# First matmuls of seven products over pairs of token groups, 512 columns each

## The chip, the core and the metric

The program runs on one core of a Trainium2 chip. A core has a matrix engine (TensorE, PE in the profile), a vector engine (VectorE, DVE), an activation engine (ScalarE, ACT), a general engine (GpSimd, POOL) and a queue engine that here only issues transfers (SyncE, SP). PE multiplies a stationary 128x128 tile, which a separate weight load (PEld) puts into the array, by a moving tile, and writes to PSUM, eight banks of 512 fp32 columns by 128 partitions. The other engines read PSUM and work on SBUF. The metric is the device time of one execution in microseconds (us), as the median of several runs.

## The reference

Batch 8, 8 heads, 576 positions, head size 64; then 4608 tokens of width 512 and 8 experts of hidden size 1024. Every expert is applied to every token; the routing only gives weights.

```python
def phi(x):
    proj = einsum('bhsd,df->bhsf', x, w_phi)
    proj = proj - max(abs(proj), axis=-1)
    return concatenate([exp(proj), exp(-proj)], -1)
q_p, k_p = phi(q), phi(k)
num = einsum('bhsf,bhfd->bhsd', q_p, einsum('bhsf,bhsd->bhfd', k_p, v))
x = (num / den).transpose(0, 2, 1, 3).reshape(4608, 512)

P = exp(x @ w_gate - max)
for _ in range(8):
    P /= P.sum(1); P /= P.sum(0); P *= N / E
for e in range(8):
    h = maximum(x @ w1[e], 0)          # the first matmul of an expert
    out += P[:, e:e+1] * (h @ w2[e])   # the second matmul
```

## The kernel before

**Stages.** The attention part ends at about 206 us and leaves x transposed in `xT` (four 128-row blocks of the width by 4608 tokens, bf16). Tokens are worked in nine groups `g` of 512. Expert 0 runs in the plain way (`up0`, `down0`), until 254 us, while DVE and PE find the routing weights `P`. Then experts 1 to 7 follow with a scheme of seven products.

**Seven products.** A product of two matrices, each cut in 2x2 blocks, is made from seven block products instead of eight; for that, sums of blocks of both factors are needed, and sums of the products. In the first matmul (`up7`) the two block columns of x are the two halves of a group, 256 tokens each. The seven products are called x1, y1, x2, w1, x3, x4, w2, each for two parts `fp` of the hidden size (x10 is x1 of part 0). `product` (L1075 to L1087) issues one of them as two blocks `i` of 128 hidden rows by two steps `k`: four matmuls of 256 columns. ACT copies a partial result from PSUM to a tile `U` (`keep`, L1112) or applies the relu (L1121); DVE adds PSUM and `U` and clips at zero (`add`, L1116, called CUSTOM_DVE_ANT_0 in the profile and ISA in the program's order). The result goes to tiles `hT`, two of 4 KB a partition for each group.

The second matmul (`down7`) has the products X1, Y1, Z1, X2, X3, Z2, X4, each of eight matmuls of 256 columns. DVE makes four sums `S` of blocks of `hT` first (`sub`, L992, four instructions of 1024 elements). Results are scaled by `P` and added to the fp32 accumulator `acc` of the group: X2, Z2 and X4 by two DVE instructions each (L1231), X1, Y1, Z1 and X3 by two ACT instructions into a tile `V` (L1243) and one POOL addition (L1246).

**Sums of x.** Four sums per group are made once, at expert 1 (`sums_x`), by DVE in instructions of 512 elements, stored to DRAM (`Xd`) and loaded again for each expert, two transfers of 256 KB a group (`load_x`, L1074), into three tiles `X`. SP issues them.

**Order.** Nothing runs in the order in which it is written. Each call of `pe`, `act`, `dve`, `pool` or `dma` records an operation with an assumed duration and its dependences; `Plan.schedule` then takes, again and again, the operation that can start first by those durations (ties by the order of writing), and fixes with it the sequence of each engine. Tiles and banks are handed out in the same pass. Each engine works through its sequence strictly, so an instruction that waits holds up all behind it on that engine. The list `ORDER` says how the second matmul of a group is written between the products of the first matmul of the next.

**The end.** For expert 7 the groups come as 8, 0, ..., 7. The last, group 7, takes its second matmul in the plain way (`down8`): 24 matmuls of 512 columns and 16 of 256, and five DVE instructions that scale and add (L1179), each followed by a store.

Of the kernel before, what the change touches and what calls it, by code (L numbers as in the profile page):

```python
# [228 lines left out]
def kernel(  # L229
# [37 lines left out]
    colw = const.tile([128, 128], FP32, name="colw")  # L267
    xT = const.tile([128, NP, N], BF16, name="xT")
    L = const.tile([128, NT, E], FP32, name="L")
# [47 lines left out]
    ring(hp, [128, 4, 512], BF16, "hT", 4)  # L317
# [22 lines left out]
    ring("s_p", [128, 1024], BF16, "T", 9)  # L340
# [3 lines left out]
    ring("s_p", [128, 2, 2, 256], BF16, "X", 3)  # L344
# [6 lines left out]
    def new(tag):  # L351
        return banks.new(int(tag[1])) if tag in ("P1", "P2") else R[tag].new()

# [395 lines left out]
    def up(w1, g, hT, fcs, n, r=(), w=()):  # L749

        for f0 in fcs[::n]:
            ph = new(f"P{n}")
            ht = hT[f0 // 4]
            for i in range(n):
                for dc in range(NP):
                    pe(512, lambda f=f0 + i, i=i, dc=dc, ph=ph: mm(
                        ph()[:, 512 * i:512 * i + 512], w1()[:, dc, f * 128:(f + 1) * 128],
                        xT[:, dc, g * 512:(g + 1) * 512], dc == 0, dc == NP - 1),
                        xkeys(g, dc) + [(w1, (f0 + i) // 2), *r], [ph, *w], [ht])
            act(512 * n, lambda f0=f0, ph=ph, ht=ht: nc.scalar.activation(  # L760
                out=ht()[:, f0 % 4:f0 % 4 + n, :].rearrange("p a b -> p (a b)"),
                in_=ph()[:, 0:512 * n], func=ACT.Relu, bias=0.0, scale=1.0),
                [ph], [(ht, f0 + i) for i in range(n)])

    def down(w2, hT, tss, r=()):
        py = new(f"P{len(tss)}")
        for i, ts in enumerate(tss):
            for fc in range(8):
                pe(512, lambda i=i, ts=ts, fc=fc: mm(
                    py()[:, 512 * i:512 * i + 512],  # L770
                    hT[fc // 4]()[:, fc % 4, ts * 128:(ts + 1) * 128],
                    w2()[:, fc, :], fc == 0, fc == 7),
                    [(hT[f // 4], f) for f in (range(8) if fc == 0 else (fc,))]
# [8 lines left out]
    def up0(g, part):  # L782
        if part == 0:
            hts[g] = [new("hT") for _ in range(2)]
# [123 lines left out]
    for d in plan.ops[:-1]:  # L908
        if any(b.ring in attn_rings for b in d.bufs):
            d.users.append(o)  # L910
            o.deps.append(d)
            o.left += 1

# [40 lines left out]
    routing()  # L954
    for i in fill:
# [3 lines left out]
    def store(g, ts, js=()):  # L959
        if len(js):  # L960
            cols = slice(256 * js[0], 256 * js[-1] + 256)
            dma("SP", len(js) << 17, 320, lambda: nc.sync.dma_start(
                out=out[g * S:g * S + SM].rearrange("(p j) d -> p j d", j=NJ)[:, ts:ts + 1, cols],
                in_=acc[g][:, ts:ts + 1, cols]),
                [("acc", g, ts, j) for j in js], [("out", g, ts, j) for j in js])
# [28 lines left out]
    def sums_w(e, w1, w2):  # L994
# [17 lines left out]
        def t(n):  # L1012
# [12 lines left out]
            k(w1, *a12) + [S[1]] + late, [S[3]])  # L1025
# [20 lines left out]
    def xq(g, i, j):  # L1046
# [3 lines left out]
    Xd = [[dram.tile([128, 4, 256], BF16, name=f"xd{g}{i}") for i in range(2)]  # L1050
          for g in range(NG)]

    def sums_x(g):
# [7 lines left out]
        for n, y, z, r in ((0, b12, b11, []), (1, b22, x(0), [0]), (2, b22, b12, []),  # L1061
                           (3, b21, x(1), [1])):
            sub(dve, 512, x(n), y, z, ALU.subtract,
                xkeys(g) + ["late"] + [(X[i // 2], i % 2) for i in r]
                + ([(X[1], "slot")] if n == 2 else []),
                [(X[n // 2], n % 2)] + ([(X[1], "slot")] if n == 0 else []))
        for i in range(2):
            dma("SP", 1 << 18, 250, lambda i=i: nc.sync.dma_start(out=Xd[g][i], in_=X[i]()),
                [(X[i], n) for n in range(2)], [("Xd", g, i)])

    def load_x(g):
        X = [new("X") for _ in range(2)]
        for i in range(2):
            dma("SP", 1 << 18, 250, lambda i=i: nc.sync.dma_start(out=X[i]().rearrange("p a b c -> p (a b) c"), in_=Xd[g][i]),  # L1074
                [("Xd", g, i)], [X[i], "order of X"])  # L1075
# [13 lines left out]
    def up7(A, g, X, hT, r0):  # L1089

        def b(n):
            f, r = {"11": (xq(g, 0, 1), []), "21": (xq(g, 1, 1), []), "22": (xq(g, 1, 0), []),
                    "t1": (lambda: X[0]()[:, 0], [X[0]]), "t2": (lambda: X[0]()[:, 1], [X[0]]),
                    "t3": (lambda: X[1]()[:, 0], [X[1]]),
                    "t4": (lambda: X[1]()[:, 1], [X[1]])}[n]
            return f, r

        x, y, w = ([new("P1") for _ in range(2)] for _ in range(3))
        u = [[new("U") for _ in range(2)] for _ in range(2)]

        def prod(bank, fp, x, y, first, more=(), takes=(), wk=()):
            f, r = A[x]
            rhs, r2 = b(y)
            product(bank[fp], lambda k, i: f()[:, k, 128 * (2 * fp + i):][:, 0:128],
                    lambda k: rhs()[:, k, :], 2, xkeys(g) + r + r2 + list(more), first, takes, wk)

        def out_(fp, i, j):

            return hT[i]()[:, 2 * fp:2 * fp + 2, 256 * j:256 * j + 256]
# [5 lines left out]
        def add(bank, fp, n, i, j):  # L1115
            dve(500, lambda: nc.vector._custom_dve(  # L1116
                ADD_SAT, out=out_(fp, i, j), in0=bank[fp]().rearrange("p (a b) -> p a b", a=2),
                in1=u[fp][n](), s0=3.0e38, s1=0.0), [bank[fp], u[fp][n]], [(hT[i], fp, j)])

        def relu(fp, i, j):  # L1120
            act(512, lambda: nc.scalar.activation(  # L1121
                out=out_(fp, i, j), in_=x[fp]().rearrange("p (a b) -> p a b", a=2),
                func=ACT.Relu, bias=0.0, scale=1.0), [x[fp]], [(hT[i], fp, j)])
# [4 lines left out]
        def x1(fp):  # L1128
            prod(x, fp, "11", "11", True, more, u[fp] + hT)
            keep(fp, 0)  # L1130

        def y1(fp):
            prod(y, fp, "12", "21", True, r0, hT)
# [6 lines left out]
        def w1(fp):  # L1140
            prod(w, fp, "s1", "t1", True, A["s4"][1] + r0, hT, [("banks", fp)])
# [10 lines left out]
        def w2(fp):  # L1152
# [5 lines left out]
            for fp in range(2)}  # L1158
# [4 lines left out]
    def down8(e, g, hT, w2):  # L1163

        for ts in (2, 3, 0, 1):
            halves_ = 2 if ts == 1 else 1
            n = DD // halves_
            for c in range(halves_):
                py, cols = new("P1"), slice(n * c, n * c + n)
                for fc in range(8):  # L1170
                    i, j = fc // 4, ts // 2
                    pe(n, lambda py=py, ts=ts, fc=fc, cols=cols, n=n: mm(
                        py()[:, 0:n], hT[fc // 4]()[:, fc % 4, ts * 128:ts * 128 + 128],
                        w2()[:, fc, cols], fc == 0, fc == 7),
                        [(hT[i], fp, j) for i in range(2) for fp in range(2)]
                        + [(w2, i, j) for i in range(2) for j in range(2)] + ["P"], [py])
                js = range(2) if n == DD else (c,)
                dve(580 * n // 512, lambda py=py, ts=ts, cols=cols, n=n:
                    nc.vector.scalar_tensor_tensor(  # L1179
                        out=acc[g][:, ts, cols], in0=py()[:, 0:n],  # L1180
                        scalar=P[:, 4 * g + ts, e:e + 1], in1=acc[g][:, ts, cols],
                        op0=ALU.mult, op1=ALU.add),
                    [py, "P"], [("acc", g, ts, j) for j in js])
                store(g, ts, js)

    def down7(e, g, hT, B7):


        def a(i, j):
            return lambda: hT[j]()[:, :, 256 * i:256 * i + 256]  # L1190

        def hk(i, j):
            return [(hT[j], fp, i) for fp in range(2)]

        late, seen = akey(g), set()
        S = [new("S") for _ in range(4)]
        S01 = dve
        sub(dve, 1024, lambda: S[2](), a(0, 0), a(1, 0), ALU.subtract, hk(0, 0) + hk(1, 0),
            [S[2]])
        sub(S01, 1024, lambda: S[0](), a(1, 0), a(1, 1), ALU.add, hk(1, 0) + hk(1, 1), [S[0]])  # L1200
        sub(S01, 1024, lambda: S[1](), lambda: S[0](), a(0, 0), ALU.subtract,
            [S[0]] + hk(0, 0), [S[1]])
        sub(dve, 1024, lambda: S[3](), a(0, 1), lambda: S[1](), ALU.subtract,
            [S[1]] + hk(0, 1), [S[3]])

        def prod(bank, lhs, y, r, first, more=()):
            f, r2 = B7[y]
            product(bank, lambda k, i: lhs()[:, k, 128 * i:128 * i + 128],
                    lambda k: f()[:, k, :], 4, r + r2 + (["P"] if e else late) + list(more), first)

        def start(bank, i, j):

            out_ = acc_part(g, i, j)
            w = [("acc", g, 2 * i + n, j) for n in range(2)]
            if (i, j) in seen:
                dve(500, lambda: nc.vector.tensor_tensor(
                    out=out_(), in0=bank().rearrange("p (a b) -> p a b", a=2), in1=out_(),
                    op=ALU.add), [bank] + late, w)
            else:
                act(512, lambda: nc.scalar.copy(  # L1220
                    out=out_(), in_=bank().rearrange("p (a b) -> p a b", a=2)),
                    [bank] + late, w)
            seen.add((i, j))

        def read(bank, i, j):

            if e == 0:
                return start(bank, i, j)
# [8 lines left out]
        def read2(bank, i, j):  # L1237

            if e == 0:
                return start(bank, i, j)  # L1240
            u = new("V")
            for n in range(2):
                act(390, lambda n=n: nc.scalar.activation(  # L1243
                    out=u()[:, n, :], in_=bank()[:, 256 * n:256 * n + 256], func=ACT.Copy,
                    bias=0.0, scale=P[:, 4 * g + 2 * i + n, e:e + 1]), [bank, "P"], [(u, n)])
# [14 lines left out]
        def X1():  # L1260
            prod(x, a(0, 0), "11", hk(0, 0), True, S[1:3])
            read2(x, 0, 0)

        def Y1():
            prod(y, a(0, 1), "21", hk(0, 1), True)
            read2(y, 0, 0)

        def Z1():
            prod(z, lambda: S[0](), "t1", [S[0]], True, S[3:4])
            read2(z, 1, 1)  # L1270

        def X2():
            prod(x, lambda: S[1](), "t2", [S[1]], False)
            read(x, 0, 1)

        def X3():
            prod(x, lambda: S[2](), "t3", [S[2]], False)
            read2(x, 1, 1)
# [71 lines left out]
```

## Time and profile before

| | |
|---|---|
| runs | median 1033.93 us (1033.42 to 1034.48, three runs) |
| the profiled execution | 1034.06 us, span of its instructions 1032.3 us |
| granted PE clock | 0.999 |
| PE busy | 1015.8 us, 98% |
| DVE busy | 822.8 us, 80% |
| ACT busy | 710.0 us, 69% |
| POOL busy | 464.8 us, 45% |

A busy time counts an instruction from its start to its end, and instructions of one engine overlap at their edges: a matmul of 256 columns lasts 273 ns in the profile, and the next one starts about 109 ns after it. Rates are therefore read from the distance of starts. The chain is what the profile finds by going back from the last instruction to whatever released each step.

### The profile page before, as it was taken

How to read it: one execution, taken by the hardware profiler on the slowest of the kernel's cores; microseconds unless marked ns; L12 is line 12 of the kernel's file. 1: busy time of each engine (PE TensorE's matmuls, PEld its weight loads, DVE VectorE, ACT ScalarE, POOL GpSimd, SP SyncE). 2: the span in 40 equal slices, each digit the busy share in tenths (PEclk: the TensorE clock that was granted, in tenths of full speed). 3: DMA queues.
4: the chain of work that ended last, by engine and by line, in shares of the span. 5: the costliest groups of instructions: out<-in, count | busy, mean ns of one | idle time of the engine just before them, and what ended most of it. 6: DMA issues, size and time to landing. Idle time of an engine off the chain costs nothing.

```text
span 1032.3 us, 24552 instructions
## 1 busy us (share of the span) xinstructions
PE 1015.8 (98%) x9526; PEld 843.5 (82%) x9526; DVE 822.8 (80%) x1628; ACT 710.0 (69%) x1569; POOL 464.8 (45%) x534
## 2 busy tenths in 40 slices
PE   7899999999999999999999999999999999999998
PEld 5666666645888888888888888888888888888886
DVE  7999998987777887778776877788777877787775
ACT  7999999835777756666666566666666656666663
POOL 5877765400244443334444443344444444434442
PEclk9999999999999999999999999999999999999999
DMA  9998995085411251115211441134111611114333
GB/s 247 182 173 145 180 165 95 11 204 135 93 49 42 50 115 41 42 49 99 70 42 43 91 83 42 42 83 93 41 45 50 123 43 42 42 46 129 113 134 123
DMA packets 105381, 93.93 MB, mean 91 GB/s; under 512 B 45408, under 2 KB 80544, under 8 KB 105264
## 3 DMA queue, kind: packets, MB, share of 16 engines
q1 hardware_dynamic: 71504, 68.44, 23.9%
q0 software_dynamic: 33680, 23.90, 16.4%
q8 instruction: 74, 1.21, 0.5%
q14 instruction: 43, 0.35, 0.1%
q10 hardware_dynamic: 80, 0.03, 0.0%
HBM read 94.98 MB, written 14.16 MB: 106 GB/s over the span
## 4 chain that ended last, share of the span: by engine, by line
PE 94%; DVE 3%; DMA 1%; ACT 1%; SPq 1%; issue 1%; POOL 0%; DVEq 0%
PE P L1084 73%; PE P L468 18%; PE P L667 1%; DMA acc<-in_q_dram 1%; DVE m L460 1%; PE P L706 1%; DMA v_r<-in_v_dram 1%; SPq L390 0%; PE P L672 0%; DVE S L992 0%; DVE hT L1116 0%; DVE acc L1231 0%; ACT k L464 0%; ACT q L464 0%; DVE xb L687 0%
## 5 line engine op out<-in xcount | busy, mean ns | idle before, releaser
L1246 POOL TENSOR_TENSOR acc<-acc,V 128x512 f32<-128x512 f32 x248 | 318.4, 1292 | 437.6 <-ACT V L1243 434.3
L1116 DVE CUSTOM_DVE_ANT_0 hT<-P,U 128x512 bf16<-128x512 f32 x378 | 255.3, 688 | 121.5 <-ACT U L1112 68.6
L1112 ACT COPY U<-P 128x512 f32<-128x512 f32 x378 | 216.4, 587 | 126.8 <-PE P L1084 121.7
L1243 ACT ACTIVATE V<-P 128x256 f32<-128x256 f32 x496 | 205.0, 473 | 131.1 <-PE P L1084 119.6
L1084 PEld LDWEIGHTS <-w 128*128 128x128 bf16 x2016 | 197.3, 98 | 23.1
L1084 PEld LDWEIGHTS <-S 128*128 128x128 bf16 x1984 | 194.1, 98 | 22.7 <-issue 0.3
L1231 DVE SCALAR_TENSOR_TENSOR acc<-P,acc 128x256 f32<-128x256 f32 x372 | 158.9, 478 | 58.2 <-PE P L1084 56.1
L1084 PEld LDWEIGHTS <-T 128*128 128x128 bf16 x1512 | 147.9, 98 | 18.0 <-issue 0.9
L1084 PEld LDWEIGHTS <-hT 128*128 128x128 bf16 x1488 | 145.5, 98 | 18.4 <-DVE hT L1116 1.0
L1084 PE MATMUL P<-X,w 128*128 128x256 bf16 x1008 | 154.3, 273 | 0.0
L1084 PE MATMUL P<-xT,w 128*128 128x256 bf16 x1008 | 151.1, 273 | 0.0
L1084 PE MATMUL P<-X,T 128*128 128x256 bf16 x1008 | 148.7, 273 | 0.0
L1084 PE MATMUL P<-w,hT 128*128 128x256 bf16 x992 | 142.2, 273 | 0.9 <-ACT V L1243 0.5
L1084 PE MATMUL P<-T,S 128*128 128x256 bf16 x1056 | 136.3, 273 | 0.1
L1084 PE MATMUL P<-w,S 128*128 128x256 bf16 x928 | 126.3, 273 | 0.0
L593 POOL TENSOR_TENSOR v<-v_m,em 128x512 bf16<-128x512 f32 x64 | 66.9, 1045 | 44.2 <-ACT em L464 40.0
L460 DVE TENSOR_REDUCE m<-P 128x4 f32<-128x512 f32 x128 | 83.8, 680 | 3.6 <-PE P L468 2.5
L992 DVE TENSOR_TENSOR S<-hT 128x1024 bf16<-128x1024 bf16 x124 | 84.2, 711 | 0.0
L1121 ACT ACTIVATE hT<-P 128x512 bf16<-128x512 f32 x126 | 72.9, 600 | 13.1 <-PE P L1084 12.3
L468 PE MATMUL P<-w,hT 128*128 128x512 bf16 (+1 forms) x328 | 79.5, 374 | 0.2 <-DVE m L460 0.2
L1084 PE MATMUL P<-xT,T 128*128 128x256 bf16 x504 | 75.5, 273 | 0.8 <-DVE hT L1116 0.8
L468 PE MATMUL P<-xT,w 128*128 128x512 bf16 x288 | 74.8, 379 | 0.3 <-ACT q L464 0.3
(97 smaller groups left out, 1097.8 us busy)
## 6 DMA issues: line engine op xcount, KB each, us to landing
X<-xd SPq DMA_DIRECT2D x126, 256.0 KB, 2.6
w<-in_moe_w_dram POOLq DMA_DIRECT2D x14, 1024.0 KB, 10.0
v_m<-in_v_dram SPq DMA_DIRECT2D x14, 512.0 KB, 4.4
out_dram<-acc SPq DMA_DIRECT2D x14, 512.0 KB, 3.1
xd<-S SPq DMA_DIRECT2D x18, 256.0 KB, 2.4
qk<-in_k_dram POOLq DMA_DIRECT2D x12, 256.0 KB, 5.6
qk<-in_q_dram POOLq DMA_DIRECT2D x12, 256.0 KB, 6.7
w<-in_moe_w_dram POOLq DMA_DIRECT2D x8, 256.0 KB, 7.7
```

Of the source, the lines that this page charges most:

```text
L460: dve(el, lambda: nc.vector.tensor_reduce(out=dst(), in_=src(), axis=AX.X, op=ALU.max, apply_absolute_value=True), r, w)
L468: nc.tensor.matmul(out_, lhsT=lhsT, rhs=rhs, start=start, stop=stop)
L593: pool(512, lambda y=y, em=em: nc.gpsimd.tensor_tensor(out=s["v"][y]()[:, :, 0:D], in0=t["v"]()[:, h0:h0 + 2].rearrange("p a (b c) -> p (a ...
L667: pe(65, lambda j=j: nc.tensor.matmul(num()[:, j, :], lhsT=s["T"][x]()[:, j % 2, 2 * h + j // 2, :], rhs=kv()[:, x, h, :], start=x == 0 an ...
L992: lambda: f.tensor_tensor(out=out_(), in0=x(), in1=y(), op=op), r, w, **kw)
L1084: pe(256, lambda i=i, k=k, z=z: nc.tensor.matmul(bank()[:, 256 * i:256 * i + 256], lhsT=lhs(k, i), rhs=rhs(k), start=first and z, stop=k = ...
L1112: act(512, lambda: nc.scalar.copy(out=u[fp][n]().rearrange("p a b -> p (a b)"), in_=x[fp]()), [x[fp]], [u[fp][n]])
L1116: dve(500, lambda: nc.vector._custom_dve(ADD_SAT, out=out_(fp, i, j), in0=bank[fp]().rearrange("p (a b) -> p a b", a=2), in1=u[fp][n](), s ...
L1121: act(512, lambda: nc.scalar.activation(out=out_(fp, i, j), in_=x[fp]().rearrange("p (a b) -> p a b", a=2), func=ACT.Relu, bias=0.0, scale ...
L1231: dve(330, lambda n=n, ts=ts: nc.vector.scalar_tensor_tensor(out=acc[g][:, ts, 256 * j:256 * j + 256], in0=bank()[:, 256 * n:256 * n + 256 ...
L1243: act(390, lambda n=n: nc.scalar.activation(out=u()[:, n, :], in_=bank()[:, 256 * n:256 * n + 256], func=ACT.Copy, bias=0.0, scale=P[:, 4 ...
L1246: pool(670, lambda: nc.gpsimd.tensor_tensor(out=acc[g][:, 2 * i:2 * i + 2, 256 * j:256 * j + 256], in0=acc[g][:, 2 * i:2 * i + 2, 256 * j: ...
```

## The change

- `up7` works on a pair of groups `p`, 1024 tokens: the block columns of x are now the two groups, 512 tokens each, and a product is four parts `fp` of two matmuls of 512 columns. Group 8 is left over and keeps the old form.
- `hT` is eight tiles of 2 KB a partition, and four more once the attention tiles are gone; a pair takes eight. Each tile holds two 128-row blocks of the hidden size of one group.
- The sums of x of a pair are four tiles of 2 KB. They are loaded into six places: a quarter of `xT` per pair that no product reads once the sums exist, the tile `early` (which held the routing's exponentials `L` and the constant `colw`), and one own tile. Each load is two issues of 128 KB. `T`, the tiles for sums of weights, go from nine to eight.
- The sums `S` of `hT` are made in eight instructions of 512 elements instead of four of 1024.
- In the last expert, `down8` is gone. The second matmuls of groups 6 and 7 both come after all first matmuls, in seven products each, written by turns (`END`); for these two groups more of the results are added by DVE, and each quarter of the output is stored when it is complete.

```diff
-    ring(hp, [128, 4, 512], BF16, "hT", 4)
+    ring(hp, [128, 2, 512], BF16, "hT", 8)
...
-    ring("s_p", [128, 2, 2, 256], BF16, "X", 3)
+    ring("s_p", [128, 2, 512], BF16, "X", 1)
+    R["X"].free = [(0.0, 5)]
+    R["X"].make = lambda i, w: (
+        xT[:, 0:2, 1024 * i:1024 * i + 512] if i < 4 else
+        early.rearrange("p (a b) -> p a b", a=2) if i == 4 else
+        late["s_p"].tile([128, 2, 512], BF16, name="X", tag=f"X_{i}"))
...
+        def load(n):
+            for k in range(2):
+                nc.sync.dma_start(out=X[n]()[:, k, :], in_=Xd[p][n][:, k, :])
+        for n in range(len(X)):
+            dma("SP", 1 << 18, 250, lambda n=n: load(n), [("Xd", p, n)], [X[n], "order of X"])
...
         def prod(bank, fp, x, y, first, more=(), takes=(), wk=()):
...
+            for k in range(2):
+                pe(512, lambda k=k: nc.tensor.matmul(
+                    bank[fp](), lhsT=f()[:, k, 128 * fp:128 * fp + 128], rhs=rhs(k),
+                    start=first and k == 0, stop=k == 1, skip_group_check=True),
...
-        sub(dve, 1024, lambda: S[2](), a(0, 0), a(1, 0), ALU.subtract, hk(0, 0) + hk(1, 0),
-            [S[2]])
...
+        def s2():
+            for h in range(2):
+                sub(dve, 512, sh(2, h), part(0, 0, h), part(1, 0, h), ALU.subtract,
+                    hk(0, 0, h) + hk(1, 0, h) + ["sums of h"], [(S[2], h)])
...
+        by_dve = ("X2", "Z2", "X4")
+        if e == E - 1 and g in (6, 7):
+            by_dve = (("X2", "X3", "X4", "Z1", "Z2") if g == 6 else ("X3", "X4", "Z1", "Z2"))
...
+    END = (
+        "aX1 aX2 aY1 aZ1 aZ2 bX1 aX3 bX2 bZ1 bY1 bX3 aX4 bX4 bZ2").split()
...
-            if e == E - 1 and g == 7:
-                down8(e, g, hT, w2)
-            else:
-                dn = down7(e, g, hT, B7)
...
+    d6, d7 = pop(), pop()
+    for n in END:
+        (d6 if n[0] == "a" else d7)(n[1:])
```

Where it moves instructions, two places matter. The first is the end of DVE's sequence. The names are those of the program: ISA is the addition that makes `hT`, `S<-hT` and `hT<-hT` are sums for the second matmul (in the last group they go into free `hT` tiles), acc_4259, acc_4260 and acc_4261 are the accumulators of groups 5, 6 and 7 before.

```order
L992 TENSOR_TENSOR S<-hT 128x1024 x2
L1116 ISA hT<-P,U 128x2x256
L992 TENSOR_TENSOR S<-S,hT 128x1024
L1116 ISA hT<-P,U 128x2x256
L992 TENSOR_TENSOR S<-hT,S 128x1024
L1116 ISA hT<-P,U 128x2x256 x2
L1231 SCALAR_TENSOR_TENSOR acc_4260<-P,acc_4260 128x256 x2
L1116 ISA hT<-P,U 128x2x256 x2
L1231 SCALAR_TENSOR_TENSOR acc_4260<-P,acc_4260 128x256 x4
L1179 SCALAR_TENSOR_TENSOR acc_4261<-P,acc_4261 128x512 x3
L1179 SCALAR_TENSOR_TENSOR acc_4261<-P,acc_4261 128x256 x2
```

The same place after the change, where acc_4270, acc_4271 and acc_4272 are groups 5, 6 and 7:

```order
L1194 ISA hT<-P,U 128x512 x2
L1305 SCALAR_TENSOR_TENSOR acc_4270<-P,acc_4270 128x256 x4
L1013 TENSOR_TENSOR S<-hT 128x512
L1013 TENSOR_TENSOR S<-S,hT 128x512
L1013 TENSOR_TENSOR S<-hT,S 128x512
L1013 TENSOR_TENSOR hT<-hT 128x512 x8
L1305 SCALAR_TENSOR_TENSOR acc_4271<-P,acc_4271 128x256 x8
L1305 SCALAR_TENSOR_TENSOR acc_4272<-P,acc_4272 128x256 x2
L1305 SCALAR_TENSOR_TENSOR acc_4271<-P,acc_4271 128x256 x2
L1305 SCALAR_TENSOR_TENSOR acc_4272<-P,acc_4272 128x256 x6
```

Before, sums stood between additions and reads of results; now eleven sums stand in one run ahead of the first read of a result of group 6.

The second place is the end of SP's sequence, with the last loads and the stores, before:

```order
L1074 DMA X<-xd_113 128x1024
L1074 DMA X<-xd_114 128x1024
L968 DMA out_dram<-acc_81 128x1024 x2
L1074 DMA X<-xd_115 128x1024
L968 DMA out_dram<-acc_4259 128x1024 x2
L968 DMA out_dram<-acc_4260 128x1024 x2
L962 DMA out_dram<-acc_4261 128x512 x3
L962 DMA out_dram<-acc_4261 128x256 x2
```

and after:

```order
L989 DMA out_dram<-acc_79 128x1024 x2
L989 DMA out_dram<-acc_80 128x1024 x2
L989 DMA out_dram<-acc_4270 128x1024 x2
L982 DMA out_dram<-acc_4271 128x2x256 x4
L982 DMA out_dram<-acc_4272 128x2x256 x2
L982 DMA out_dram<-acc_4272 128x256 x2
L982 DMA out_dram<-acc_4272 128x2x256
```

The loads of sums now end well ahead of the stores, the output of groups 6 and 7 goes out in quarters, and the last store has 128x2x256 elements where it had 128x256.

318 lines of the change are left out of this document (192 added, 126 removed).

## The prediction

> **What bounds the kernel now.** I read the page first, then the stretches, then the chain. The busy line and the chain's shares:
>
> ```profile
> span 1032.3 us, 24552 instructions
> PE 1015.8 (98%) x9526; PEld 843.5 (82%) x9526; DVE 822.8 (80%) x1628; ACT 710.0 (69%) x1569; POOL 464.8 (45%) x534
> PE 94%; DVE 3%; DMA 1%; ACT 1%; SPq 1%; issue 1%; POOL 0%; DVEq 0%
> ```
>
> PE is the bound. Whether it has gaps where the change acts is told by the stretches (start:end, length, then busy time of PE, PEld, DVE, ACT, POOL with counts, clock, DMA share, GB/s), and by who PE waited for between 254 and 360 us:
>
> ```profile
> 254.00:360.00 106.00, 104.21 (x946) 92.11 (x944) 80.16 (x138) 81.22 (x165) 40.67 (x33) 1.00 0.22 56
> 360.00:1021.50 661.50, 661.50 (x6062) 592.92 (x6060) 505.96 (x905) 413.66 (x865) 285.62 (x226) 1.00 0.28 70
> 1021.50:1033.00 11.50, 7.15 (x43) 3.86 (x40) 4.88 (x9) 0.00 (x0) 1.28 (x2) 0.90 0.48 182
> ...
> PE P L1084 <- DVE hT L1116: 1.2, 3, 0.8
> PE P L1084 <- ACT V L1243: 0.5, 1, 0.5
> ```
>
> From 360 us to the last group PE never stands still, so only fewer or shorter matmuls help there. Before that 106.00 - 104.21 = 1.8 us are lost at the start of the experts. The chain in order of time (start, length, what) gives the rates, with a run of 512-column matmuls of expert 0 from the timeline:
>
> ```profile
> 356.62 665.11 PE P L1084 x6091
> 1021.72 6.94 PE P L468 x40
> 1028.68 0.48 DVE acc L1179
> ...
> 246.12 8.15 PE L468 MATMUL P<-w,hT 128*128 128x512 bf16 x37
> ...
> L468 PE MATMUL P<-w,hT 128*128 128x512 bf16 x312 | 77.7, 379 | 0.2 <-DVE m L460 0.2
> L1084 PEld LDWEIGHTS <-w 128*128 128x128 bf16 x2016 | 197.3, 98 | 23.1
> ```
>
> A 256-column matmul takes 665.11/6091 = 109.2 ns from start to start; a 512-column one (8.15 - 0.38)/36 = 215.9 ns, each with a weight load of its own in both cases. Weight loads (98 ns) are hidden, so halving their number is worth nothing by itself.
>
> **Term 1, wider first matmuls: -4.0 us.** 7 experts x 4 pairs x 7 products x 4 parts x 2 steps = 1568 matmuls of 512 columns replace 3136 of 256. Each saves 2 x 109.2 - 215.9 = 2.5 ns, together 4.0 us. An error of 0.01 us in the run of 37 moves this by 0.4: 3.5 to 4.4. All of it lies on the path, since PE is full.
>
> [...]
>
> **Term 2, the last group in seven products: -0.8 us.** The 40 plain matmuls took 6.94 us; 56 of 256 columns take 56 x 0.1092 = 6.12.
>
> **Term 3, the end of DVE's sequence: +2.7 us.** The durations on DVE and POOL, first by group, then as runs in the timeline:
>
> ```profile
> L1246 POOL TENSOR_TENSOR acc<-acc,V 128x512 f32<-128x512 f32 x248 | 318.4, 1292 | 437.6 <-ACT V L1243 434.3
> L1116 DVE CUSTOM_DVE_ANT_0 hT<-P,U 128x512 bf16<-128x512 f32 x378 | 255.3, 688 | 121.5 <-ACT U L1112 68.6 <-PE P L1084 51.4
> L1243 ACT ACTIVATE V<-P 128x256 f32<-128x256 f32 x496 | 205.0, 473 | 131.1 <-PE P L1084 119.6 <-issue 7.6 <-POOL acc L1246 2.1
> L1231 DVE SCALAR_TENSOR_TENSOR acc<-P,acc 128x256 f32<-128x256 f32 x372 | 158.9, 478 | 58.2 <-PE P L1084 56.1
> ...
> 207.29 0.76 DVE L992 TENSOR_TENSOR S<-xT 128x512 bf16<-128x512 bf16 x2 [0.39 <-DVE xT L709]
> 207.97 0.42 DVE L992 TENSOR_TENSOR S<-xT,S 128x512 bf16<-128x512 bf16 x1
> 259.50 1.29 DVE L1116 CUSTOM_DVE_ANT_0 hT<-P,U 128x512 bf16<-128x512 f32 x2
> 262.61 1.28 DVE L992 TENSOR_TENSOR S<-hT 128x1024 bf16<-128x1024 bf16 x2
> 531.48 1.27 POOL L1246 TENSOR_TENSOR acc<-acc,V 128x512 f32<-128x512 f32 x1 [0.53 <-ACT V L1243]
> 531.54 1.75 DVE L992 TENSOR_TENSOR S<-hT 128x1024 bf16<-128x1024 bf16 x1
> 533.21 1.65 DVE L1231 SCALAR_TENSOR_TENSOR acc<-P,acc 128x256 f32<-128x256 f32 x4
> 534.78 0.67 DVE L992 TENSOR_TENSOR S<-hT 128x1024 bf16<-128x1024 bf16 x1
> ```
>
> From start to start an addition takes 0.60 us (1.29 - 0.69), a read of a result 0.39 ((1.65 - 0.48)/3), a sum of 1024 elements 0.60 (1.28 - 0.68), one of 512 elements 0.34 (0.76 - 0.42). The pair at 531.5 us shows one more thing: a sum that starts 0.06 us after a POOL addition takes 1.75 us instead of 0.67. DVE stood still until POOL was done: 1.08 us.
>
> In the middle the halved sums cost DVE 8 x 0.34 - 4 x 0.60 = 0.32 us a group, 17 us in the 54 groups of the long stretch (661.5 over 112 x 0.1092). Its idle time there is 661.5 - 506.0 = 155 us, which hides them. If that cover went, PE would wait for `hT`.
>
> At the end nothing is left to hide behind. Take the last first matmul as zero. By the order DVE then has two additions (1.2), four reads of group 5 (1.6), eleven sums (3.7) and two reads of X2 of group 6 (0.9): 7.4 us. PE has nine products of eight matmuls before X3 of group 6, which must wait for that reading, since it goes into the same bank: 9 x 8 x 0.1092 = 7.9 us. So there are 0.5 us to spare, without POOL. But POOL's additions for X1 and Y1 of group 6 and one for group 7 fall in: X1 is the fifth of the nine, done at 4.4, scaled by ACT 0.9 later (0.47 for one half and nearly as much for the other), so POOL adds from about 5.3 to 9. DVE's sums run from 2.8 to 6.5 if nothing stops them. The last ones meet POOL. If each sum that finishes lets the next POOL addition in first, three meet: 3 x 1.08 - 0.5 = 2.7 us of standing PE. Bounds: 0 if POOL comes after the sums, 0.6 for one meeting. I take three, because POOL's additions come close together there and `S3` needs the earlier sums, so DVE cannot pass them. Behind the sums wait all reads of groups 6 and 7; behind those, PE.
>
> [...] With one meeting instead of three the sum would be 2.1 us lower.
>
> **Term 4, after the last matmul: +0.7 us.** One read of 0.48 us followed it (1028.68 above); now the last bank has two, 0.39 more. The last store is 256 KB instead of 128:
>
> ```profile
> X<-xd SPq DMA_DIRECT2D x126, 256.0 KB, 2.6
> w<-in_moe_w_dram POOLq DMA_DIRECT2D x14, 1024.0 KB, 10.0
> out_dram<-acc SPq DMA_DIRECT2D x14, 512.0 KB, 3.1
> out_dram<-acc SPq DMA_DIRECT2D x10, 128.0 KB, 2.4
> out_dram<-acc SPq DMA_DIRECT2D x3, 256.0 KB, 2.4
> ```
>
> By these rows between 0 and 3.1 - 2.4 = 0.7 more, as three other stores go out in the 2 us ahead of it; I take 0.3.
>
> **Term 5, the start of the experts: 0.** The 1.8 us there may go (a pair gives PE more to do before it needs a second matmul) or double (the sums of x, 16 instructions of 1024 and four of 512, now end in loads into `xT`). DVE's total for them falls, 36 x 0.34 = 12.2 us against 16 x 0.60 + 4 x 0.34 = 11.0. Between -1.8 and +1.8 I take the middle.
>
> Loads of sums cost nothing as long as they land in time. SP issues twice as many; one issue in the chain's first rows:
>
> ```profile
> 1.26 0.46 SPq L390
> ```
>
> That is 0.5 us more for each tile. A pair's third and fourth tile come free after x2 and w1 of the second half of the pair before. After w1, by `ORDER`, six products of first matmuls (6 x 0.43) and four of second (4 x 0.87) stand ahead of the next x1: 6.1 us, against 2.6 + 0.5.
>
> Sum: -4.0 - 0.8 + 2.7 + 0.7 = -1.4 us, from the profiled 1034.06 to 1032.7. The median of the runs is 0.13 lower than the profiled one: **1032.5 us**.
>
> **Rivals.**
> - *The end is clean.* The sums slip past POOL, or meet it once. For it: the 0.5 us to spare, and assumed durations that can shift POOL by some tenths. Terms: -4.0 - 0.8 + 0.3 + 0.7 = -3.8, 1030.1 us.
> - *DVE and POOL collide in the middle.* Eight sums a group instead of four can meet POOL's four additions. PE needs 112 x 0.1092 + 56 x 0.2159 = 24.3 us a pair, DVE 12 x 0.60 + 16 x 0.34 + 12 x 0.39 = 17.3; it decides from six meetings of 1.08 a pair on, or from one just ahead of X1. Against it: the long stretch has no gap although meetings like the one at 531.5 occur. If a third of 28 pairs lose 0.5 us: +4.7, 1037.2 us, slower.
> - *Wide matmuls bring nothing.* If the second step into a whole bank cost what two narrow ones do, term 1 is zero: 1036.5 us. Against it stand the 37 matmuls.
> - *Sums of x come late.* While weights load (10.0 us), a load of sums may take several us more than 2.6 and use up the 6.1. A loss of 1 us in each of six experts gives 1038.5 us.
>
> **How the numbers follow.** Three meetings 0.50 (own range 1031.3 to 1034.5), clean end 0.26, middle collisions 0.10, no gain from width 0.06, late loads 0.08. The likeliest gives 1032.5. The lower end, 1029.4, takes in the clean end with a gain at the start; the upper, 1036.4, leaves out most of the last two and of the collisions, about 0.15. A change under 0.2%, 2.1 us, can hardly be told from none: faster means below 1031.9. That is 0.24 of the clean end and 0.08 of the likeliest: 0.32. Slower, above 1036.0: 0.18 from the last three. The rest, 0.50, is the same.
>
> **What would show it.** Term 1: first matmuls at 216 ns from start to start. Term 2: 56 short matmuls in place of the 40. Term 3: sums of 512 elements near 1.5 us in the last 15 us, and a gap of PE of some 2 to 3 us before X3 of group 6, ended by DVE's read of `acc`. Term 4: two reads and a 256-KB store after the last matmul. A PE busy less than the whole between 360 and 1010 us would make the prediction wrong by the second or the last rival, a cadence of 218 by the third.

## The result

The changed kernel takes 1036.82 us in the median of 13 runs (1035.11 to 1038.23), the kernel before 1033.67 us on the same chip (13 runs, 1032.80 to 1035.43). The ratio is 1.0028 with a 95% interval of 1.0020 to 1.0037: slower by some 3 us, where 1032.5 was forecast. The profiled execution took 1037.74 us with a span of 1036.0, against a span of 1032.3 before.

The page of the changed kernel, its busy line, and three stretches (columns as in the prediction; 254 to 360 us is the start of the experts):

```profile
span 1036.0 us, 21792 instructions
PE 1008.2 (97%) x7856; PEld 692.1 (67%) x7974; DVE 877.0 (85%) x1875; ACT 706.7 (68%) x1571; POOL 467.4 (45%) x535
...
254.00:360.00 106.00, 104.83 (x708) 70.08 (x718) 84.29 (x172) 80.71 (x166) 38.51 (x31) 1.00 0.28 66
...
1020.00:1023.00 3.00, 0.26 (x3) 0.09 (x2) 3.00 (x5) 0.46 (x2) 1.65 (x2) 1.00 0.24 87
1023.00:1026.30 3.30, 3.30 (x17) 2.29 (x17) 1.52 (x4) 0.00 (x0) 0.00 (x0) 0.50 0.00 0
```

PE is busy for 7.6 us less than before, and yet the span grew. The last two rows show most of the reason: 3 us in which PE hardly works, and behind them 3.3 us in which it is granted half its clock, 17 matmuls where 30 would fit. (118 records of matmuls are missing in this trace, 7856 beside 7974 weight loads, so busy times of PE are a little low: they are no measure of the work saved, and a busy share under 100% alone proves no gap here. Gaps below are read from the starts.)

The whole balance, from the starts of matmuls in both traces:

| step | us | read from |
|---|---|---|
| wider first matmuls | -4.0 | a run of 22 from start to start, below |
| last group in seven products | -0.8 | 56 short matmuls for 40 plain ones |
| start of the experts | -1.4 | gaps there: 2.6 us before, 1.2 now |
| changes of experts | +3.3 | four gaps of 0.74, one of 0.29 |
| further into experts 4 to 6 | +0.4 | three gaps of 0.14 |
| PE standing in the last 20 us | +3.4 | one gap of 2.90, two of 0.28 and 0.26 |
| half clock behind the gap | +1.9 | 18 matmuls at 213 ns instead of 109 |
| after the last matmul | +0.9 | 3.64 us before, 4.58 now |
| sum | +3.7 | span: +3.7 |

The first row is the chain's run of 512-column matmuls: (4.91 - 0.38)/21 = 215.7 ns. The others show whom PE waited for (between 254 and 360 us, then between 360 and 1008 us):

```profile
260.43 4.91 PE P L1164 x22
...
PE P L1130 <- DVE hT L1194: 0.3, 1, 0.3
PE P L1164 <- ACT U L1190: 0.2, 1, 0.2
...
PE P L1164 <- DVE acc L1305: 2.3, 4, 0.6
```

The view counts a wait from the modelled end of the matmul before, 0.16 us (0.38 - 0.22) after the next one could have started, so four waits of 0.57 us are four gaps of 0.74. All lie just behind a change of experts. Here is the first, in the timelines of PE, DVE and POOL:

```profile
464.72 0.38 PE L1164 MATMUL P<-xT,w 128*128 128x512 bf16 x1
465.67 0.38 PE L1164 MATMUL P<-xT,w 128*128 128x512 bf16 x1 [0.57 <-DVE acc L1305]
...
461.84 2.21 DVE L1013 TENSOR_TENSOR w<-w 128x1024 bf16<-128x1024 bf16 x1
463.97 1.65 DVE L1305 SCALAR_TENSOR_TENSOR acc<-P,acc 128x256 f32<-128x256 f32 x4
...
460.18 0.79 POOL L378 DMA_DIRECT2D w<-in_moe_w_dram  x1 [2.18 <-PE P L1130]
461.00 2.49 POOL L1319 TENSOR_TENSOR acc<-acc,V 128x512 f32<-128x512 f32 x2
```

Read it from below: POOL issues a weight load for 0.79 us, which makes its next two additions late; they run one behind the other until 463.49. DVE's sum of weights, 0.68 us by itself, comes in during the first and is held until the second is done. Four reads of `acc` stand behind it, and PE needs a bank that these free.

In the kernel before, the sequences at the same change of experts fell otherwise. The issue stood behind the two additions, and the sums of weights (0.68 us each) ahead of the additions and behind them (DVE, then POOL):

```profile
464.61 0.68 DVE L992 TENSOR_TENSOR T<-w 128x1024 bf16<-128x1024 bf16 x1
469.43 0.68 DVE L992 TENSOR_TENSOR w<-w 128x1024 bf16<-128x1024 bf16 x1
...
465.43 2.58 POOL L1246 TENSOR_TENSOR acc<-acc,V 128x512 f32<-128x512 f32 x2 [6.05 <-ACT V L1243]
467.94 0.79 POOL L362 DMA_DIRECT2D w<-in_moe_w_dram  x1
```

And the end, in the same three timelines:

```profile
1019.36 0.82 PE L1130 MATMUL P<-T,hT 128*128 128x256 bf16 x6
1022.92 1.79 PE L1130 MATMUL P<-T,S 128*128 128x256 bf16 x8 [2.74 <-DVE acc L1305]
1030.35 1.03 PE L1130 MATMUL P<-T,hT 128*128 128x256 bf16 x8
...
1016.09 5.99 DVE L1013 TENSOR_TENSOR hT<-hT 128x512 bf16<-128x512 bf16 x8
1022.00 1.65 DVE L1305 SCALAR_TENSOR_TENSOR acc<-P,acc 128x256 f32<-128x256 f32 x4
1031.42 0.88 DVE L1305 SCALAR_TENSOR_TENSOR acc<-P,acc 128x256 f32<-128x256 f32 x2 [0.18 <-PE P L1130]
...
1017.64 2.74 POOL L1319 TENSOR_TENSOR acc<-acc,V 128x512 f32<-128x512 f32 x2 [3.53 <-ACT V L1315]
1020.54 1.26 POOL L1319 TENSOR_TENSOR acc<-acc,V 128x512 f32<-128x512 f32 x1
```

Eight sums that need 2.8 us (2.76 in the kernel with later weight sums, below) take 5.99: three of them meet three POOL additions. X3 of group 6 starts 2.90 us late. Its eight matmuls then take 1.79 us instead of 1.03: that is the half clock.

### The profile page after: what moved, and what is told of

Read it like the earlier page. It is cut to its first block, busy times and chain, and to the rows that moved or that the text cites. A ratio compares the mean times of both kernels' runs of the same rounds, so it can differ in the third digit from the quotient of the medians.

```text
span 1036.0 us, 21792 instructions
## 1 busy us (share of the span) xinstructions
PE 1008.2 (97%) x7856; PEld 692.1 (67%) x7974; DVE 877.0 (85%) x1875; ACT 706.7 (68%) x1571; POOL 467.4 (45%) x535
## 4 chain that ended last, share of the span: by engine, by line
PE 84%; DVE 5%; issue 1%; ACT 1%; DVEq 0%; ACTq 0%
PE P L1130 39%; PE P L1164 31%; PE P L484 13%; DVE acc L1305 1%; DVE hT L1194 1%; PE P L683 1%; DVE w L1013 1%; DVE hT L1013 1%; PE P L722 0%; DVE S L1013 0%; ACT q L480 0%; DVE m L476 0%; PE P L688 0%; ACT U L1190 0%; ACT hT L776 0%
## 5 line engine op out<-in xcount | busy, mean ns | idle before, releaser
L1315 ACT ACTIVATE V<-P 128x256 f32<-128x256 f32 x498 | 217.8, 476 | 127.0 <-PE P L1130 123.4
L1164 PE MATMUL P<-xT,w 128*128 128x512 bf16 x674 | 191.3, 379 | 3.6 <-DVE acc L1305 2.3
L1130 PEld LDWEIGHTS <-hT 128*128 128x128 bf16 x1544 | 151.1, 98 | 57.7 <-DVE hT L1194 0.7
L1164 PE MATMUL P<-xT,T 128*128 128x512 bf16 x550 | 158.1, 379 | 1.8
L1164 PEld LDWEIGHTS <-w 128*128 128x128 bf16 x896 | 87.6, 98 | 62.0 <-issue 0.7
L1013 DVE TENSOR_TENSOR S<-hT 128x512 bf16<-128x512 bf16 x248 | 103.1, 433 | 19.2 <-PE P L1130 18.4
L1164 PEld LDWEIGHTS <-T 128*128 128x128 bf16 x672 | 65.7, 98 | 58.9 <-issue 4.2
L484 PE MATMUL P<-xT,w 128*128 128x512 bf16 x271 | 71.7, 379 | 0.9 <-ACT q L480 0.3
L484 PE MATMUL P<-w,hT 128*128 128x512 bf16 x272 | 69.7, 379 | 0.8 <-DVE m L476 0.2
L1130 PE MATMUL P<-T,hT 128*128 128x256 bf16 x528 | 70.4, 273 | 0.1
L480 ACT ACTIVATE q<-P 128x512 bf16<-128x512 f32 x128 | 69.4, 637 | 1.2 <-PE P L484 0.9
```

The lines of the kernel that those rows point to most:

```text
L480: act(el, lambda: nc.scalar.activation(out=dst(), in_=src(), func=ACT.Exp, bias=0.0, scale=scale), r, w)
L484: nc.tensor.matmul(out_, lhsT=lhsT, rhs=rhs, start=start, stop=stop)
L1013: lambda: f.tensor_tensor(out=out_(), in0=x(), in1=y(), op=op), r, w, **kw)
L1130: pe(256, lambda i=i, k=k, z=z: nc.tensor.matmul(bank()[:, 256 * i:256 * i + 256], lhsT=lhs(k, i), rhs=rhs(k), start=first and z, stop=k = ...
L1164: pe(512, lambda k=k: nc.tensor.matmul(bank[fp](), lhsT=f()[:, k, 128 * fp:128 * fp + 128], rhs=rhs(k), start=first and k == 0, stop=k == ...
L1315: act(390, lambda n=n: nc.scalar.activation(out=u()[:, n, :], in_=bank()[:, 256 * n:256 * n + 256], func=ACT.Copy, bias=0.0, scale=P[:, 4 ...
```

## The experiments

Ratios are to the kernel before on the same chip, with 95% intervals. Differences to the changed kernel (1036.82 us) are between runs on different chips: the kernel before took 1033.67 us beside the changed kernel and 1033.76, 1033.94 and 1034.18 beside the experiments, so they are uncertain by some tenths.

**The first POOL addition behind the last sum.** A copy of one column of `V` onto itself, which stands behind the last sum in DVE's sequence, holds back POOL's first addition of group 6, and with it all that follow.

```diff
+            if (e, g, name) == (E - 1, 6, "X1"):
+                dve(1, lambda: nc.vector.tensor_copy(out=u()[:, 0, 0:1], in_=u()[:, 0, 0:1]),
+                    ["sums of h"], [(u, 0), (u, 1)])
             pool(670, lambda: nc.gpsimd.tensor_tensor(
...
```

> Theory: the 2.9 us of standing PE before X3 of group 6 come from three POOL additions that fall between DVE's last sums, and the 3.4 us at clock 0.5 behind it come from the standing itself. Here the first POOL addition of group 6 waits until the last sum is written, so no sum can meet one. The last sums then take 0.42 us each instead of 1.49, PE's gap before X3 falls from 2.9 to under 1 us, the clock stays at 1.0: -2.2 and -1.9, against some +0.7 because POOL's additions now end later: about 1033.4 us. Rival, DVE simply has too much to do there: the sums run one behind the other without POOL and the gap is still 2 to 3 us, 1036 to 1037 us. Rival, the half clock has nothing to do with the gap: the gap goes, the clock still falls to 0.5 near 1023 us, about 1035.3 us.

Measured: 1033.48 us (1032.83 to 1034.47), ratio 0.9997 (0.9989 to 1.0006). All PE waits from 1008 us on, and the clock where it was 0.50:

```profile
PE P L1130 <- DVE acc L1305: 0.5, 1, 0.5
...
1023.00:1026.30 3.30, 2.77 (x26) 2.27 (x25) 2.62 (x8) 1.57 (x4) 2.56 (x3) 1.00 0.85 290
```

Both the gap and the half clock are gone, and 3.3 us with them, as the first theory had it. DVE's list of work alone was not too long.

**The last group as before.** `down8` of the kernel before, written for the new tiles, in place of the seven products of group 7. The results of group 6 are then added as those of every other group are.

```diff
-    d6, d7 = pop(), pop()
-    for n in END:
-        (d6 if n[0] == "a" else d7)(n[1:])
+    d6 = pop()
+    for n in ORDER:
+        if len(n) == 2:
+            d6(n)
+    down8(E - 1, 7, queue[0][2], w2)
```

> The last group is multiplied as before (40 plain matmuls of 512 columns, its stores by 128 KB), beside the seven products of group 6; pairs and wide first matmuls stay. Theory: the whole loss at the end goes, that is gaps of 2.9 + 0.5 us, 1.9 us of half clock and 1.0 us after the last matmul, and the 0.8 us that the seven products saved come back: -5.5 us, about 1031.3. What then is left against the kernel before (1033.7) is what the wide matmuls brought, less some 3 us of gaps at the changes of experts. Rival, the loss lies in the middle and the end only moves it: no change or a few tenths more, 1036.5 to 1037.5.

Measured: 1033.19 us, ratio 0.9994 (0.9986 to 1.0003), 3.6 us below the changed kernel; its profiled span, 1031.3, is 4.7 below. The loss was at the end for the most part. The 5.5 expected counted on 1.0 us after the last matmul, of which 0.2 came back; the rest of it is in the spans, and the medians differ by less because the profiled execution of the changed kernel lies 0.9 above its median. Its four gaps at the changes of experts stand as they did (2.4 us in the waits).

**Sums of the second weight later.** For experts 2 to 6 the four DVE sums of w2 may only be made in the first pair of the expert.

```diff
-        late = late + ["sums of w1"]
...
+        return A, lambda: sums_w2(e, w2, T, q, k, t)
+    def sums_w2(e, w2, T, q, k, t):
+        late = ["late", "P" if e == 1 else "late" if e == E - 1 else "mid", "sums of w1"]
...
-                out=u[fp][n]().rearrange("p a b -> p (a b)"), in_=x[fp]()), [x[fp]], [u[fp][n]])
+                out=u[fp][n]().rearrange("p a b -> p (a b)"), in_=x[fp]()), [x[fp]],
+                [u[fp][n]] + (["mid"] if (fp, n) == (1, 1) else []))
```

> For experts 2 to 6 the four sums of the second weight are made later, beside the first pair of the expert, instead of at the change of experts. Theory: PE's gaps of 0.74 us at 465, 575, 685 and 796 us come from one such sum (1024 elements, in place) that stands behind two POOL additions for 2.2 us, with reads of results queued behind it; they fall to 0.25 us or less, -2.0 us or a little more: about 1034.7. Rival, POOL's issue of the weight load (0.79 us) delays POOL's additions and PE waits for these in whatever order DVE works: the gaps stay, 1036.8.

Measured: 1032.98 us, ratio 0.9999 (0.9989 to 1.0009): 3.8 us below the changed kernel, and for another reason than the one given. DVE's row at the same change of experts, the waits from 350 to 1008 us, then DVE and POOL at the end:

```profile
461.74 1.94 DVE L1013 TENSOR_TENSOR S<-hT,S 128x512 bf16<-128x512 bf16 x1
...
PE P L1168 <- DVE acc L1310: 1.6, 5, 0.4
...
1014.90 2.76 DVE L1013 TENSOR_TENSOR hT<-hT 128x512 bf16<-128x512 bf16 x8
...
1016.45 4.91 POOL L1324 TENSOR_TENSOR acc<-acc,V 128x512 f32<-128x512 f32 x3 [3.53 <-ACT V L1320]
```

With the weight sum gone, a sum of `hT` of 0.42 us takes its place behind the two additions and needs 1.94: gaps of 0.46 to 0.48 remain, and a new one of 0.58 stands at 355 us. So it was not that sum alone: another sum in its place meets POOL's two additions in a row as well. The middle gained 0.5 us net. The rest came from the end, which nothing had touched: in this execution the eight sums went through in 2.76 us and POOL waited for them. Nine of the 11 runs lie between 1031.74 and 1033.63, two at 1036.49 and 1037.18.

**Matmuls in place of the pause.** Thirteen matmuls of 512 columns into an unread bank, ahead of X3 of group 6.

```diff
+        def filled(mm_, f, w):
+            for _ in range(13 if f else 0):
+                nc.tensor.matmul(psum[:, 3584:4096], lhsT=w()[:, 0, 0:128], rhs=w()[:, 1, :],
+                                 start=True, stop=True, skip_group_check=True)
+            mm_()
```

> Thirteen further matmuls of 512 columns (2.8 us) stand ahead of X3 of group 6, into a bank that nobody reads; all else is as in the changed kernel. Theory: the three meetings of sums and additions stay, X3 starts when it did, but PE does not stand still, so the clock stays at 1.0 and the 18 matmuls behind it take 109 ns instead of 213: -1.9 us, about 1034.9. Rival, the clock falls for another reason (the end of the program, few other engines at work): it is 0.5 again behind X3, 1036.8 or some tenths more.

Measured: 1035.79 us, ratio 1.0019 (1.0010 to 1.0028). The stretch behind X3 ran at clock 1.00 (row below). But in the profiled execution the sums went by ahead of POOL, so X3 was not late and the 2.8 us were simply added. With no pause of PE in this execution, the clock only says that it does not fall there for another reason, such as the end of the program; the 1.9 us are not shown by this run.

```profile
1023.00:1026.30 3.30, 3.30 (x29) 2.67 (x28) 1.57 (x4) 0.00 (x0) 0.38 (x1) 1.00 0.23 79
```

**Weight loads later.** POOL issues the loads of experts 3 to 7 in the first pair of the expert before instead of at the change.

```diff
-                r, [(w, i, j) for i in range(2) for j in range(2)])
+                r + ([("mid", e - 1)] if e > 2 else []),
+                [(w, i, j) for i in range(2) for j in range(2)])
...
-                out=u[fp][n]().rearrange("p a b -> p (a b)"), in_=x[fp]()), [x[fp]], [u[fp][n]])
+                out=u[fp][n]().rearrange("p a b -> p (a b)"), in_=x[fp]()), [x[fp]],
+                [u[fp][n]] + ([("mid", ex)] if (p, fp, n) == (0, 1, 1) else []))
```

> The loads of the weights of experts 3 to 7 are issued by POOL a few us later, in the first pair of the expert before, instead of right at the change of experts; nothing else is moved by hand. [...] Theory B, DVE's sums at the change of experts are simply too many: the gaps stay at 0.7. At the end the sums either meet POOL as in the changed kernel (then about 1035.0 in all) or go by ahead of it as they did in most runs of the kernel with later weight sums (then about 1031.5).

Measured: 1035.12 us (1033.57 to 1035.91), ratio 1.0007 (0.9999 to 1.0016), 1.7 below the changed kernel. The waits from 360 to 1008 us, POOL and DVE at the first of these changes, and the end:

```profile
PE P L1165 <- DVE acc L1307: 0.6, 4, 0.2
...
459.79 2.49 POOL L1321 TENSOR_TENSOR acc<-acc,V 128x512 f32<-128x512 f32 x2 [2.58 <-ACT V L1317]
461.04 1.79 DVE L1014 TENSOR_TENSOR w<-w 128x1024 bf16<-128x1024 bf16 x1
...
1013.60 5.99 DVE L1014 TENSOR_TENSOR hT<-hT 128x512 bf16<-128x512 bf16 x8
...
1020.42 1.03 PE L1131 MATMUL P<-T,S 128*128 128x256 bf16 x8 [2.74 <-DVE acc L1307]
...
1020.30:1023.60 3.30, 3.18 (x30) 2.85 (x30) 2.67 (x8) 0.30 (x1) 0.00 (x0) 1.00 0.08 29
```

The edit was made because POOL's issue (0.79 us) seemed to be what sets its two additions one behind the other, and gaps of 0.3 us or less were expected. The gaps of 0.74 us fall to 0.31 to 0.32, so the size was right and theory B is out. Half of the reason is wrong, though: the two additions stand one behind the other without the issue too, and the weight sum is still held by both. They only start 0.4 us earlier against the matmuls beside them, the sum then takes 1.79 us instead of 2.21, and the gap shrinks by the same 0.42. So the issue is worth 1.7 us at four changes, and two additions in a row with a DVE sum among them keep the other 0.3 of each gap.

The end shows the same meetings and the same gap of 2.90 us, and yet clock 1.00 behind it, X3 in 1.03 us. The runs fall into two sets: five of 1033.57 to 1034.27 with a mean clock of 0.999 or more, six of 1035.12 to 1035.91 with 0.997 or 0.998. It fits that the same pause cost 1.5 us of clock in one set and none in the other, but the one trace is of the first set, and the kernel before has runs at 0.998 too.

**All together, twice.** Weight sums and weight loads later, with POOL's wait at the end, or with the last group as before.

> Three edits together: the four sums of the second weight later, the weight loads later, and the first POOL addition of the last two groups behind the last sum. Theory: no gap over 0.3 us is left between 360 and 1008 us (3.4 us less standing than in the changed kernel), the end as in the kernel with that wait alone (1033.5): about 1030.3 us, faster than the kernel before by 3.4. Rival, the sums moved into the first pair meet other POOL additions there and PE waits there instead: 1032.5 to 1033.5.

> The same two edits at the change of experts, with the last group multiplied as before (plain, 40 matmuls). Theory: 1033.2 of the kernel with the last group undone alone, less 3.4: about 1029.8 us. Rival as for the kernel with the wait: 1032 to 1033.

Measured: 1030.93 us, ratio 0.9973 (0.9963 to 0.9984), and 1030.31 us, ratio 0.9964 (0.9951 to 0.9978). Both beat both kernels. With the last group as before the view of waits shows none of PE from 360 us on, and the last stretch is nearly full:

```profile
360.00:1008.00 648.00, 644.13 (x4565) 453.43 (x4635) 542.30 (x1105) 405.67 (x854) 285.63 (x223) 1.00 0.27 68
1008.00:1024.50 16.50, 16.04 (x117) 11.45 (x117) 10.52 (x22) 5.11 (x12) 6.25 (x5) 1.00 0.40 151
```

Against the versions with the end mended alone these are 2.6 and 2.9 us better (3.4 expected). Of the 3.7 us of gaps between 360 and 1008 us 3.0 are gone in both traces; the one of 0.29 and the three of 0.14 are still there, too short for the view. With the last group as before the 3.6 us to the kernel before (3.8 in the spans) are, to within some tenths, what the wide matmuls bring (4.0) and the start of the experts (1.4), less these 0.7 us of gaps and 0.7 after the last matmul.

**Narrow matmuls.** Each first matmul of a pair as two of 256 columns, each with its weight load.

```diff
-            for k in range(2):
-                pe(512, lambda k=k: nc.tensor.matmul(
-                    bank[fp](), lhsT=f()[:, k, 128 * fp:128 * fp + 128], rhs=rhs(k),
+            for c in range(2):
+                for k in range(2):
+                    z = c == 0 and k == 0
+                    pe(256, lambda k=k, c=c, z=z: nc.tensor.matmul(
+                        bank[fp]()[:, 256 * c:256 * c + 256],
+                        lhsT=f()[:, k, 128 * fp:128 * fp + 128],
+                        rhs=rhs(k)[:, 256 * c:256 * c + 256],
...
```

> The changed kernel with every first matmul of a pair issued as two of 256 columns instead of one of 512, each with a weight load of its own, as before the change; pairs, tiles and the last groups stay. Theory: 1568 x 2.5 ns come back, +4.0 us, about 1040.8; the gaps at the changes of experts and at the end stay within some tenths of what they were. Rival, the width brought nothing because other engines set the pace: no change, 1036.8.

Measured: 1041.29 us, ratio 1.0073 (1.0056 to 1.0091), 4.5 above the changed kernel in the medians. The gap before X3 stayed at 2.74 us in the view, but the clock did not fall in the profiled execution, so the medians do not compare like with like. The spans do: 1038.7 against 1036.0 is 2.7 more, although 1.9 us of half clock are gone, and 0.6 of it are longer gaps and a later end. That leaves 4.0 us for the width. Term 1 is right.

**The parts by themselves.** Sums against additions, and pauses of PE, in a program of their own.

> Not the computation but its parts by themselves, the output is left unfilled. First 24 times: DVE runs ten sums of 512 elements one behind the other, and a POOL addition of 128x512 comes in between, each time 13 ns later. [...] Theory B, they take turns: the addition starts behind the sum that is running, and the next sum takes 1.5 us. [...] Then TensorE runs 80 matmuls, stands still for k copies by ACT (k from 2 to 12, about 0.5 us each) and goes on: if standing still for some 3 us is what halves the clock, the matmuls behind the longer pauses take about 430 ns instead of 216 for some 3.4 us, those behind pauses of 1 to 1.5 us do not.

First the pauses. Rows of PE: start, time of the whole run of matmuls, count, and the pause ahead of it in brackets; then two stretches with their clock.

```profile
286.02 17.43 PE L56 MATMUL P<-W 128*128 128x512 bf16 x78 [3.26 <-ACT U L58]
307.33 18.90 PE L56 MATMUL P<-W 128*128 128x512 bf16 x78 [3.89 <-ACT U L58]
381.48 20.07 PE L56 MATMUL P<-W 128*128 128x512 bf16 x79 [6.40 <-ACT U L58]
430.44 17.21 PE L56 MATMUL P<-W 128*128 128x512 bf16 x78 [1.37 <-ACT U L58]
450.49 19.11 PE L56 MATMUL P<-W 128*128 128x512 bf16 x79 [2.85 <-ACT U L58]
472.87 18.76 PE L56 MATMUL P<-W 128*128 128x512 bf16 x78 [3.26 <-ACT U L58]
...
286.00:289.40 3.40, 3.33 (x15) 1.00 0.00 0
451.90:455.20 3.30, 3.30 (x10) 0.51 0.00 0
```

Without a pause that matters 78 matmuls take 17.2 to 17.4 us. Pauses of 1.37 and 2.63 us cost nothing; one of 2.85 cost 1.7; one of 3.26 nothing the first time and 1.3 the second; from 3.89 on each cost something, up to 2.7. The half clock starts up to 1.4 us after the matmuls have started again and then lasts 2.8 to 3.5 us, or up to 5.4 behind the longer pauses (estimated as twice the time lost). So a pause near 3 us halves the clock or does not, and by what is not visible in the program. The shortest pause that it followed was 2.85 us here and 2.74 us in the changed kernel, as the views count them.

Then POOL's additions that come in during ten sums:

```profile
10.38 1.39 POOL L41 TENSOR_TENSOR acc<-acc,V 128x512 f32<-128x512 f32 x1 [9.94 <-ACT V L38]
15.14 4.07 POOL L41 TENSOR_TENSOR acc<-acc,V 128x512 f32<-128x512 f32 x1 [3.37 <-ACT V L38]
20.09 1.37 POOL L41 TENSOR_TENSOR acc<-acc,V 128x512 f32<-128x512 f32 x1 [0.88 <-ACT V L38]
24.86 4.04 POOL L41 TENSOR_TENSOR acc<-acc,V 128x512 f32<-128x512 f32 x1 [3.40 <-ACT V L38]
```

In strict turns, 12 and 12 times: the addition gets in behind the sum that is running or the next one, or it waits for the tenth. These look like the two ends seen above, 5.99 and 2.76 us for eight sums. The arrival moved by 13 ns from round to round and had no say. In 24 further rounds three sums came in during three additions, and they took turns in all of them, about 1.46 us each for the later ones.

**Which of the two.** The same rounds alone, with one or two further meetings behind each, and with a pause.

> Not the computation but one part by itself, the output is left unfilled. In the run of the parts, ten DVE sums one behind the other and a POOL addition that comes in between gave two outcomes in strict turns: in every first round the addition got in after one to three sums, in every second it waited for the tenth. Here 16 rounds alone, 16 with one further meeting (one sum that comes during an addition) behind each round, 16 with two, 16 with a pause of some 2 us and no meeting. Theory A, the side that is let in changes with every meeting: turns in the first, third and fourth part, one and the same outcome in all 16 rounds of the second. [...] Theory C, it is the phase in which the addition arrives: outcomes repeat with the eight phases in each part.

The additions of the rounds, by part (count, then total and mean in ns): the first alone, the last with a pause (14 of its 16 rounds are in the stretch):

```profile
L42 POOL TENSOR_TENSOR acc<-acc,V 128x512 f32<-128x512 f32 x16 | 42.2, 2636 | 45.2 <-ACT V L39 45.2
...
L42 POOL TENSOR_TENSOR acc<-acc,V 128x512 f32<-128x512 f32 x14 | 19.9, 1423 | 93.4 <-ACT V L39 93.4
```

Alone: turns again, 1.3 and 4.0 us. In the other three parts the addition was let in 48 times out of 48. Theories A and C fall. What goes with it in all 88 rounds of both programs is whether DVE had stood idle between the ten sums before and the round's own: then POOL got in (68 times), and where DVE had come straight from one run of sums to the next, it waited (20 times). In the kernels themselves this does not tell the ends apart, since DVE's sequence is alike up to 10 ns in both; what decides there stays open.

## Why the prediction was wrong

- **Term 1 (-4.0) was right**: 215.7 ns from start to start, and 4.0 us of span when it is undone. The rival that width brings nothing is out.
- **Term 2 (-0.8) was right** in size. As a step it does not pay: with the last group as before the kernel is no slower (1033.19 against 1033.48 with POOL held back).
- **Term 3 (+2.7) was right in mechanism and size**: three meetings, eight sums that take 3.2 us longer, X3 late by 2.9, and 0.5 of small gaps beside it. The clean end that got 0.26 exists too. By their times it came in most runs of one variant (later weight sums). Which of the two comes was not known ahead and is not explained, so it was luck that three meetings came and not none.
- **Term 3 was cut short: the step that failed first.** It counted PE's standing time and stopped there. Behind a pause of 2.9 us PE also lost half its clock for 3.3 us, 1.9 us more, in the profiled execution. The mean clock points to the same in some eight of the 13 runs: 0.996 or 0.997, where the kernel before never fell under 0.998 in the 57 runs beside the experiments. The trace of before holds no pause of PE over 1.7 us, so it could not show this.
- **The cover in the middle: the step that failed most.** "Its idle time there is 661.5 - 506.0 = 155 us, which hides them" is an average. At the changes of experts a sum came to stand among two POOL additions in a row, which a weight load to be issued had made late, and the reads that PE waited for stood behind that sum: 3.3 us in five gaps, and 0.4 in three more. The rival for the middle had the mechanism and nearly the price (4.7, slower), with a chance of 0.10. It looked for meetings spread over a third of the pairs; nearly all of the loss was at one place of each expert, where the cover was thin. It reckoned 1.08 us a meeting and passed by that two additions in a row held a sum for both (2.21 us instead of 0.68), and that the issue of a load (0.79 us) made POOL late. That the halved sums of `hT` had to bring this about is not shown: the sum that was held at these changes is one of weights, which the kernel before has too, and what differs is the place that it got in the sequences.
- **Term 4 (+0.7)** measured 0.9: the last store goes out behind five others, 3.4 us of issues on SP.
- **Term 5 (0)** measured -1.4, within its bounds. Late loads of sums, the other rival, cost nothing that shows.

By terms: forecast -1.4, against +3.7 in the spans. The gaps between 360 and 1008 us (+3.7) and the clock (+1.9) were missing, the start gave 1.4 back, and the rest is small.

## What to carry to other kernels

DVE's idle time of 155 us over the long stretch before did not hide the sums at the changes of experts (3.3 us lost): look for where an engine's queue is longest (here the change of experts, with a load that POOL issues in 0.79 us) and cost the added instructions there. Price a standstill of PE of about 3 us with the half clock that may follow it, some 1.3 to 1.9 us here, and take a result that hangs on which of DVE and POOL gets in first for a toss (the same eight sums took 2.76 or 5.99 us). Where DVE sums and POOL additions must not meet, a dependence that holds one of them back is cheap: one copied column was worth 3.3 us.

## What was not expected of the hardware

- A run of ten DVE sums one behind the other kept POOL out to its end (4.07 us for an addition that takes 1.26) or let it in behind the first or second (1.3 to 1.6 us). In the two programs of parts an idle time of DVE ahead went with being let in in all 88 rounds; the phase of arrival had no say.
- A pause of PE of 2.9 us led to 3.3 us at half clock in the profiled execution of the changed kernel and to none in those of two variants with the same pause; in the program of parts a pause of 3.26 us did it the second time and not the first. The two sets of runs 1.5 us apart, by mean clock, fit this.
- Two POOL additions in a row kept a DVE sum out for both at the changes of experts: 2.21 us instead of 0.68 for the sum of weights.
